# Loading the first chunk's weight words into two more buffers, an earlier residual load, and a chunk's closing steps one per unit, in an attention, DFT and feed-forward kernel

## The chip, the cores and the metric

The kernel runs on one core of one Trainium2 chip. The metric is the device time of one execution in microseconds (us). The core has a tensor engine (PE, with its own weight loads, PEld), a vector engine (DVE), a scalar engine (ACT), GpSimd (POOL), and SyncE (SP), on whose queue every transfer of this kernel is issued. Each engine works its own instructions in the order in which they stand, and waits at one whose inputs or buffers are not ready.

## The reference

q, k and v are (8, 12, 448, 64); the weights are 768 x 3072 and 3072 x 768.

```python
scores = scale * np.matmul(q, k.transpose(0, 1, 3, 2)) - np.log(S)
attn = 1.0 / (1.0 + np.exp(-scores))
x = attn @ v                      # heads side by side: (8, 448, 768)
X = np.fft.fft(np.fft.fft(x, axis=1), axis=2)
u = x + np.real(X).astype(np.float32)
un = (u - mean(u)) / np.sqrt(var(u) + 1e-06)      # over the last axis
out = (u + np.maximum(un @ w_ch1, 0.0) @ w_ch2).astype(np.float32)
```

The weights arrive as float64 words, that is, as pairs of 32-bit words, and are made into pairs of float16 tiles (a high part and a low part) on the chip.

## The kernel before

The 8 x 448 = 3584 tokens of the feed-forward part are seven chunks of 512. The work has four stages on the time line.

**Attention and DFT**, up to about 456 us, are not touched.

**The first chunk** (c = 0, 456 to 715 us): for each of the 24 blocks of 128 hidden units (f) there is `up_proj` (18 matmuls into `psh`), `evac` (ACT writes `hh`, L545; DVE writes `hl`, L546) and `down_proj` of the block before (24 matmuls into the six banks `po`). Beside it the weights are made. The list `order` names 48 weight blocks; `prep_step(k, n)` makes block k in four parts: SP loads the words of a later block into a buffer `wr` (L373), ACT takes an absolute value (`wt`, L382), DVE makes four passes (L384 to L392), ACT writes the high part (L400), SP stores `wt` to `t_dram` (L401), and DVE writes the low part one step later (L403). Two such steps stand in each block f. There are three `wr` buffers, and at step k the words of block k + 2 are loaded.

**The second chunk** (c = 1, 715 to 931 us) has the same three parts, and beside them two others. `combine(i, p, n)` makes 24 combined weight tiles for the fast chunks: n = 0 loads `cb` from `t_dram` (L619, in the `wr` buffers too), n = 1 is four adds on DVE (L627), n = 2 the high part `ch` on ACT (L631), n = 3 the low part `cl` on DVE (L636), n = 4 six stores. `made_at` says in which block each part of tile j stands: loads in f - 1, adds and `ch` in f, `cl` and stores in f + 1, with f = 1 + j - (j > 8) - (j > 16), so that blocks 9 and 16 have two tiles. `fast_norm` normalizes the rows of the third chunk, in two passes of 12 blocks each (f 0 to 11 and 11 to 22): statistics, 16 short DVE steps for the root, transposes on PE (`pst`, in blocks 6 to 8 and 17 to 19, each in one of the two buffers of `psh`), copies to `U` (L676) and to `ut` (L688, L692). `residual(c, g)` loads the rows `ur` that are added at the end (L570), again into the `wr` buffers; `finish` adds them to the banks `po` (L578) when the last `down_proj` has filled them, and stores the result (L582).

**The fast chunks** (c = 2 to 6, from 931 us) work in units: seven products up (`fast_up`, `psf`, L771), seven down (`fast_down`, `pso`, L822), in turn; `fast_unit` runs one product and then what `todo` holds for this unit. `later(d, fn)` puts a step d units ahead. Weights come by `load_w` into `ws` (L699), each in a unit of its own before it is used. A down product is added to `acc` on DVE (L831). In the last group of a chunk `fast_finish` follows each down product: eleven steps for each half of the tokens (seven adds, `add`, L846; four `put`, L850, of which two issue a store to `out`, L856). They stand in the unit of the product itself, so all eleven lie in six units in a row.

After each group `pin()` fixes the order on every engine as it is written.

Of the kernel before, what the change touches and what calls it, by code (L numbers as in the profile page):

```python
# [11 lines left out]
I32 = mybir.dt.int32  # L12
# [11 lines left out]
DM = 768  # L24
# [34 lines left out]
def spectral_attention_ffn(tc, q, k, v, w1, w2, cd, cs, ident_in, out):  # L59
# [8 lines left out]
    with ExitStack() as top:  # L68
# [19 lines left out]
        if True:  # L88
# [279 lines left out]

            def prep_w(i, f, n):

                if n == 0:
                    prep[i, f] = r = wpre.tile([128, DM, 2], I32, tag="wr", name="wr", bufs=3)
                    nc.sync.dma_start(  # L373
                        r.rearrange("p n w -> p (n w)"), (w1, w2)[i][:, f * 2 * DM:(f + 1) * 2 * DM])
                    return
# [30 lines left out]
            def prep_step(k, n):  # L406

                for d, m in (((2, 0), (-1, 4)), ((1, 1),), ((0, 2),), ((0, 3),))[n]:
                    if k + d < len(order) and (k + d, m) not in prepped:
                        prepped.add((k + d, m))  # L410
                        prep_w(*order[k + d], m)
# [108 lines left out]
        with ExitStack() as fast, ExitStack() as st, ExitStack() as early:  # L520
            un_pool = fast.enter_context(tc.tile_pool(name="un_pool", bufs=1))
            up = fast.enter_context(tc.tile_pool(name="up", bufs=2))
# [180 lines left out]
            for j in range(NFC):  # L703
                f = 1 + j - (j > 8) - (j > 16)
                made_at.setdefault(f - 1, []).append((j, 0))
                made_at.setdefault(f, []).extend((j, n) for n in (1, 2))
                made_at.setdefault(f + 1, []).extend((j, n) for n in (3, 4))
# [7 lines left out]
            for c in range(NPLAIN):  # L715
                for f in range(NFC):
                    if (c, f) not in hs:
                        up_proj(c, f)
                    for n in range(2):
# [4 lines left out]
                        if n == 0 and (c or f):  # L724
                            evac(c, f)
                    if c == NPLAIN - 1:
# [5 lines left out]
                    if f in (NFC - 3, NFC - 2) and c < NPLAIN - 1:  # L732
                        residual(c, f - NFC + 3)
                    if f == NFC - 1 and c == NPLAIN - 1:
                        residual(c, 0)
                        residual(c, 1)
# [104 lines left out]
            def fast_finish(c, tp, no):  # L841
# [16 lines left out]
                for x in {2: ((add, 2, 1), (put, 2, 0, 0)), 6: ((add, 6, 1),), 7: ((add, 7, 6),),  # L858
                          4: ((add, 4, 7), (put, 4, 1, 0)), 5: ((add, 7, 5), (add, 6, 5), (put, 7, 1, 1)),
                          3: ((add, 3, 6), (put, 3, 0, 1))}.get(no, ()):  # L860
                    later(0, lambda x=x: x[0](*x[1:]))
# [97 lines left out]
```

## Time and profile before

| what | value |
|---|---|
| time, median of 3 runs | 1811.45 us (1807.61 to 1819.85) |
| the profiled execution | 1808.63 us, its span 1806.8 us |
| PE busy | 1670.1 us (92%) |
| DVE busy | 1297.8 us (72%) |
| ACT busy | 603.1 us (33%) |
| DMA queue | 61.5% of 16 engines' span, 393.19 MB |
| mean granted PE clock | 0.977 |

The span is the time from the first to the last instruction of the profiled execution. A busy share is a mean over stages that differ, so the rows below go stage by stage. A wait in square brackets is idle time of that engine just before the row, with what ended it.

### The profile page before, as it was taken

The numbers are of one execution on the slowest core, as the hardware profiler recorded it, in microseconds if no ns is written. First come the engines' busy times: TensorE is split into PE (matmuls) and PEld (weight loads), VectorE is DVE, ScalarE is ACT, GpSimd is POOL, SyncE is SP. The second block draws the span as 40 slices with busy tenths as digits, with TensorE's granted clock in tenths as the row PEclk, the third lists the DMA queues.
The fourth block names the chain that finished last, engine by engine and source line by source line (L and its number), as shares of the span: only waits on it lengthen the run. The fifth ranks groups of instructions, "written<-read, shape, count | busy, mean of one in ns | idle before, by whom it ended". The sixth has DMA issues, their size and how long they took to land. (4 is left out here: it accounts for less than half of the span.)

```text
span 1806.8 us, 27683 instructions
## 1 busy us (share of the span) xinstructions
PE 1670.1 (92%) x10996; PEld 1069.6 (59%) x10996; DVE 1297.8 (72%) x2481; ACT 603.1 (33%) x767; POOL 193.6 (11%) x220
## 2 busy tenths in 40 slices
PE   8999999987777778999879999999999999999997
PEld 4555545543533334555447777677777767776774
DVE  4445576656777776567656888788868887887667
ACT  5444444434333332133224332333133323232221
POOL 4534344334000000000000000000000000000000
PEclk9999999998999999999989999999999999999999
DMA  7666676654666665588887563756476546556551
GB/s 243 214 207 220 222 229 219 207 167 117 217 211 211 211 212 195 182 280 309 294 303 266 227 245 145 280 202 231 152 284 224 217 178 254 216 205 249 215 223 62
DMA packets 109139, 394.95 MB, mean 219 GB/s; under 512 B 23521, under 2 KB 49362, under 8 KB 93522
## 3 DMA queue, kind: packets, MB, share of 16 engines
q1 hardware_dynamic: 109010, 393.19, 61.5%
q8 instruction: 86, 1.41, 0.3%
q14 instruction: 43, 0.35, 0.1%
HBM read 316.08 MB, written 73.92 MB: 216 GB/s over the span
## 5 line engine op out<-in xcount | busy, mean ns | idle before, releaser
L771 PE MATMUL psf<-ut,ws 128*128 128x256 f16 x3780 | 425.4, 274 | 21.4 <-DMA ws<-w_dram 11.7
L822 PE MATMUL pso<-ws,H 128*128 128x384 f16 x2520 | 423.9, 326 | 4.5 <-DVE X L777 1.8
L771 PEld LDWEIGHTS <-ws 128*128 128x128 f16 x3780 | 370.8, 98 | 74.2 <-DMA ws<-w_dram 14.8
L822 PEld LDWEIGHTS <-H 128*128 128x128 f16 x2520 | 246.3, 98 | 160.8 <-issue 5.4
L136 ACT ACTIVATE a<-sc 112x900 f32<-112x900 f32 x192 | 166.8, 918 | 157.0 <-PE sc L132 156.9
L831 DVE TENSOR_TENSOR acc<-pso,acc 128x384 f32<-128x384 f32 x350 | 183.6, 550 | 18.8 <-PE pso L822 18.8
L796 ACT ACTIVATE F<-F 128x1024 f32<-128x1024 f32 x60 | 63.5, 1058 | 357.1 <-DVE F L777 357.1
L557 PE MATMUL po<-w2h,hh 128*128 128x512 f16 (+1 forms) x384 | 131.8, 343 | 52.0 <-ACT hh L545 51.3
L152 PE MATMUL av<-a,vr 112*64 112x450 f32 x768 | 171.1, 568 | 3.8 <-DVE xT L161 3.8
L777 DVE TENSOR_TENSOR H<-F,H 128x1024 f16<-128x1024 f32 x120 | 129.5, 1087 | 48.1 <-ACT H L806 48.1
L538 PE MATMUL psh<-ut,w1h 128*128 128x512 f16 x504 | 151.2, 382 | 3.0 <-DVE hl L546 3.0
L557 PEld LDWEIGHTS <-hh 128*128 128x128 f16 x768 | 76.6, 102 | 108.6 <-ACT hh L545 61.1
L777 DVE TENSOR_TENSOR F<-X,psf 128x256 f32<-128x256 f32 x240 | 96.8, 419 | 51.8 <-PE psf L771 48.0
L557 PE MATMUL po<-w2h,hl 128*128 128x512 f16 (+1 forms) x384 | 130.8, 341 | 1.9
L806 ACT ACTIVATE H<-F 128x1792 f16<-128x1792 f32 x60 | 101.8, 1697 | 88.7 <-DVE F L777 88.7
L557 PE MATMUL po<-w2l,hh 128*128 128x512 f16 (+1 forms) x384 | 131.2, 342 | 0.0
L161 DVE TENSOR_SCALAR xT<-av 128x450 f32<-128x450 f32 x48 | 30.1, 626 | 136.2 <-PE av L152 136.2
L777 DVE TENSOR_TENSOR F<-F 128x256 f32<-128x256 f32 x240 | 91.2, 422 | 24.5 <-ACT F L796 20.5
L132 PE MATMUL sc<-qh,kh 64*112 64x450 f32 x384 | 82.2, 424 | 18.0 <-ACT a L136 13.4
L546 DVE SCALAR_TENSOR_TENSOR hl<-psh,hh 128x512 f16<-128x512 f32 x48 | 33.1, 690 | 90.5 <-ACT hh L545 90.5
L152 PEld LDWEIGHTS av<-a,vr 112*64 112x64 f32 x768 | 47.7, 139 | 82.7 <-issue 67.8
L538 PE MATMUL psh<-ut,w1l 128*128 128x512 f16 x252 | 96.1, 382 | 0.0
(89 smaller groups left out, 1954.9 us busy)
## 6 DMA issues: line engine op xcount, KB each, us to landing
ws<-w_dram SPq DMA_DIRECT2D x120, 1344.0 KB, 8.8
wr<-w_in SPq DMA_DIRECT2D x96, 768.0 KB, 4.9
t_dram<-wt SPq DMA_DIRECT2D x48, 384.0 KB, 2.3
cb<-t_dram SPq DMA_DIRECT2D x24, 768.0 KB, 5.3
qr<-q_in SPq DMA_DIRECT2D x48, 225.0 KB, 3.7
kr<-k_in SPq DMA_DIRECT2D x48, 224.0 KB, 3.4
vr<-v_in SPq DMA_DIRECT2D x24, 448.0 KB
w_dram<-ch SPq DMA_DIRECT2D x24, 384.0 KB, 5.8
```

Source lines behind the costliest of these rows:

```text
L132: nc.tensor.matmul(ps[:CP, j, :SQ], split[g, 1, kn][h, c * CP:(c + 1) * CP], split[g, 0, qn][h], start=(n == 0), stop=(n == 2))
L136: nc.scalar.activation(a, ps[:CP, :, :SQ], AF.Sigmoid, bias=-math.log(S), scale=1.0 / math.sqrt(D))
L152: nc.tensor.matmul(ps[j * D:(j + 1) * D, :SQ], vr[:, c, h * D:(h + 1) * D], a[:, j], start=(c == 0), stop=(c == 3))
L538: nc.tensor.matmul(hs[c, f], l[f][:, m], r[:, m], start=(m == n == 0), stop=(m == NCC - 1 and n == 2))
L546: nc.vector.scalar_tensor_tensor(out=hl, in0=ps, scalar=0.0, in1=hh, op0=ALU.max, op1=ALU.subtract)
L557: nc.tensor.matmul(po[n][:, at:at + hi - lo], l[:, cols], r[f][:, lo:hi], start=(f == 0 and m == 0 and at == 0), stop=(f == NFC - 1 and m ...
L771: nc.tensor.matmul(ps[:, :TH], w[:, x, a, m * 128:(m + 1) * 128], ut[y][:, b, m], start=(m == n == 0), stop=(m == n == 2))
L777: nc.vector.tensor_tensor(out=o, in0=x, in1=y, op=op)
L796: nc.scalar.activation(F[:, 0:4], F[:, 0:4], AF.Relu)
L806: nc.scalar.activation(hts[P][:, 0], F[:, 1:8], AF.Copy)
L822: nc.tensor.matmul(ps[:, :384], H[:, x, a, tp * 128:(tp + 1) * 128], w[:, y, b], start=(j == n == 0), stop=(j == 1 and n == 2))
L831: later(0, lambda: nc.vector.tensor_tensor(out=to, in0=ps[:, :384], in1=to, op=ALU.add))
```

## The change

It has four edits. Two more buffers, one tile called `spare`, are made in `un_pool`, which stands empty until the second chunk; blocks k >= 8 of the weight list with k % 5 > 2 load into them, and `prep_step` issues a load as soon as the block that held its buffer is done, up to four blocks ahead. In the second chunk `made_at` has four blocks with two tiles (5, 8, 11 and 14) in place of two (9 and 16), so the last tile is done two blocks sooner. The residual of the second chunk is loaded in blocks 21 and 22, ahead of the other steps of the block, and no longer in block 23. The closing steps of fast chunks 2 to 5 stand one to a unit in the eleven units after the last down product; those of the last chunk stay.

```diff
--- before.py
+++ after.py
@@ -366,10 +366,26 @@
             for f in range(NFC):
                 order += [(1, f)] + [(0, f + NPRE)] * (f + NPRE < NFC)
 
+            spare = []
+
+            def in_spare(k):
+                return k >= 8 and k % 5 > 2
+
+            def loadable(k, done):
+
+                here = [j for j in range(k) if in_spare(j) == in_spare(k)]
+                n = 2 if in_spare(k) else 3
+                return len(here) < n or here[-n] < done
+
             def prep_w(i, f, n):
 
                 if n == 0:
-                    prep[i, f] = r = wpre.tile([128, DM, 2], I32, tag="wr", name="wr", bufs=3)
+                    k = order.index((i, f))
+                    if in_spare(k):
+                        r = spare[0][:, k % 5 - 3]
+                    else:
+                        r = wpre.tile([128, DM, 2], I32, tag="wr", name="wr", bufs=3)
+                    prep[i, f] = r
                     nc.sync.dma_start(
                         r.rearrange("p n w -> p (n w)"), (w1, w2)[i][:, f * 2 * DM:(f + 1) * 2 * DM])
                     return
@@ -405,7 +421,12 @@
 
             def prep_step(k, n):
 
-                for d, m in (((2, 0), (-1, 4)), ((1, 1),), ((0, 2),), ((0, 3),))[n]:
+                loads = []
+                for d in range(2, 5):
+                    if not loadable(k + d, k):
+                        break
+                    loads.append((d, 0))
+                for d, m in ((*loads, (-1, 4)), ((1, 1),), ((0, 2),), ((0, 3),))[n]:
                     if k + d < len(order) and (k + d, m) not in prepped:
                         prepped.add((k + d, m))
                         prep_w(*order[k + d], m)
@@ -519,6 +540,7 @@
 
         with ExitStack() as fast, ExitStack() as st, ExitStack() as early:
             un_pool = fast.enter_context(tc.tile_pool(name="un_pool", bufs=1))
+            spare.append(un_pool.tile([128, 2, DM, 2], I32, tag="U", name="spare"))
             up = fast.enter_context(tc.tile_pool(name="up", bufs=2))
             wp = early.enter_context(tc.tile_pool(name="wp", bufs=1))
             ps_h = st.enter_context(tc.tile_pool(name="ps_h", bufs=2, space=PSUM))
@@ -701,7 +723,7 @@
 
             norm_at, made_at = {}, {}
             for j in range(NFC):
-                f = 1 + j - (j > 8) - (j > 16)
+                f = 1 + j - (j > 4) - (j > 8) - (j > 12) - (j > 16)
                 made_at.setdefault(f - 1, []).append((j, 0))
                 made_at.setdefault(f, []).extend((j, n) for n in (1, 2))
                 made_at.setdefault(f + 1, []).extend((j, n) for n in (3, 4))
@@ -723,17 +745,14 @@
                             slot += 1
                         if n == 0 and (c or f):
                             evac(c, f)
+                    if f in (NFC - 3, NFC - 2):
+                        residual(c, f - NFC + 3)
                     if c == NPLAIN - 1:
                         for j, n in made_at.get(f, ()):
                             combine(j % 2, j // 2, n)
                     if c == NPLAIN - 1:
                         for tp, n in norm_at.get(f, ()):
                             fast_norm(NPLAIN, tp, n, ps_h)
-                    if f in (NFC - 3, NFC - 2) and c < NPLAIN - 1:
-                        residual(c, f - NFC + 3)
-                    if f == NFC - 1 and c == NPLAIN - 1:
-                        residual(c, 0)
-                        residual(c, 1)
                     if prev is not None:
                         down_proj(*prev)
                     prev = (c, f)
@@ -855,10 +874,15 @@
                     elif n == 1:
                         nc.sync.dma_start(out[r0:r0 + 128, :], u[:, k])
 
-                for x in {2: ((add, 2, 1), (put, 2, 0, 0)), 6: ((add, 6, 1),), 7: ((add, 7, 6),),
-                          4: ((add, 4, 7), (put, 4, 1, 0)), 5: ((add, 7, 5), (add, 6, 5), (put, 7, 1, 1)),
-                          3: ((add, 3, 6), (put, 3, 0, 1))}.get(no, ()):
-                    later(0, lambda x=x: x[0](*x[1:]))
+                steps = {2: ((add, 2, 1), (put, 2, 0, 0)), 6: ((add, 6, 1),), 7: ((add, 7, 6),),
+                         4: ((add, 4, 7), (put, 4, 1, 0)), 5: ((add, 7, 5), (add, 6, 5), (put, 7, 1, 1)),
+                         3: ((add, 3, 6), (put, 3, 0, 1))}
+                if c == NCK - 1:
+                    for x in steps.get(no, ()):
+                        later(0, lambda x=x: x[0](*x[1:]))
+                elif no == 3:
+                    for n, x in enumerate(x for k in (2, 6, 7, 4, 5, 3) for x in steps[k]):
+                        later(1 + n, lambda x=x: x[0](*x[1:]))
 
             def fast_unit(fn, *args):
                 fn(*args)
```

**SP's queue, the end of the second chunk.** `ur` is the residual, `ch`, `cl`, `w2h`, `w2l`, `w1h` and `w1l` are sources of stores of combined weights, `ws` the fast chunks' weights. Before:

```order
L699 DMA ws<-w_dram 128x5376
L649 DMA w_dram<-ch 128x1536
L650 DMA w_dram<-w2h_4500 128x768
L651 DMA w_dram<-w2h_4499 128x384
L649 DMA w_dram<-cl 128x1536
L650 DMA w_dram<-w2l_4521 128x768
L651 DMA w_dram<-w2l_4520 128x384
L570 DMA ur<-u_dram 128x2x768 x2
L582 DMA y_out<-ur 128x2x768 x2
L699 DMA ws<-w_dram 128x5376 x5
```

Now:

```order
L721 DMA ws<-w_dram 128x5376
L592 DMA ur<-u_dram 128x2x768
L671 DMA w_dram<-ch 128x1536
L672 DMA w_dram<-w2h_4503 128x768
L673 DMA w_dram<-w2h_4502 128x384
L671 DMA w_dram<-cl 128x1536
L672 DMA w_dram<-w2l_4524 128x768
L673 DMA w_dram<-w2l_4523 128x384
L592 DMA ur<-u_dram 128x2x768
L721 DMA ws<-w_dram 128x5376
L604 DMA y_out<-ur 128x2x768 x2
L721 DMA ws<-w_dram 128x5376 x5
```

The two residual loads stood one after the other behind the last stores; now the first stands ahead of the last tile's six stores, and the second behind them.

**SP's queue, the end of the first fast chunk.** `y_out` is the output. Before:

```order
L839 DMA ur<-u_dram 128x768 x2
L699 DMA ws<-w_dram 128x5376 x4
L856 DMA y_out<-ur 128x768 x2
L699 DMA ws<-w_dram 128x5376 x2
L856 DMA y_out<-ur 128x768 x2
L699 DMA ws<-w_dram 128x5376 x2
L659 DMA U<-u_dram 128x768 x2
```

Now:

```order
L858 DMA ur<-u_dram 128x768 x2
L721 DMA ws<-w_dram 128x5376 x6
L875 DMA y_out<-ur 128x768 x2
L721 DMA ws<-w_dram 128x5376 x2
L875 DMA y_out<-ur 128x768 x2
L681 DMA U<-u_dram 128x768 x2
```

Each pair of output stores has moved behind two more weight loads.

**DVE, blocks 4 to 6 of the second chunk** (`U` is the rows' scaling in block 4, `hl` begins a block). Before:

```order
L323 TENSOR_SCALAR U<-U,mv 128x768 x2
L546 SCALAR_TENSOR_TENSOR hl<-psh,hh 128x512
L636 SCALAR_TENSOR_TENSOR cl<-cb,wsc,ch 128x1536
L627 TENSOR_TENSOR cb<-cb 128x384 x4
L546 SCALAR_TENSOR_TENSOR hl<-psh,hh 128x512
L636 SCALAR_TENSOR_TENSOR cl<-cb,wsc,ch 128x1536
L627 TENSOR_TENSOR cb<-cb 128x384 x4
```

Now:

```order
L323 TENSOR_SCALAR U<-U,mv 128x768 x2
L568 SCALAR_TENSOR_TENSOR hl<-psh,hh 128x512
L658 SCALAR_TENSOR_TENSOR cl<-cb,wsc,ch 128x1536
L649 TENSOR_TENSOR cb<-cb 128x384 x8
L568 SCALAR_TENSOR_TENSOR hl<-psh,hh 128x512
L658 SCALAR_TENSOR_TENSOR cl<-cb,wsc,ch 128x1536 x2
L649 TENSOR_TENSOR cb<-cb 128x384 x4
```

Block 5 has two sets of four adds, and block 6 two low parts.

## Rows read from the trace of the kernel before

**Rows 1.** Windows: length; busy PE, PEld, DVE, ACT, POOL; PE clock; DMA share; GB/s.

```profile
456.00:715.00 259.00, 203.00 (x987) 102.40 (x987) 198.50 (x263) 89.92 (x116) 2.93 (x2) 0.93 0.61 207
715.00:931.00 216.00, 210.46 (x1137) 111.89 (x1136) 140.51 (x232) 61.77 (x72) 0.00 (x0) 0.99 0.79 277
```

**Rows 2.** Waits, 480 to 715 us: total us, times, longest.

```profile
PE po L557 <- ACT hh L545: 51.3, 20, 7.8
...
ACT wt L382 <- DMA wr<-w_in: 4.5, 3, 2.9
```

**Rows 3.** Waits of PE, 735 to 931 us.

```profile
PE psh L538 <- DVE hl L546: 3.0, 1, 3.0
PE pst L675 <- ACT U L676: 2.5, 2, 2.3
```

**Rows 4.** Timelines, 925 to 949 us: start, us, engine, instruction, [idle before].

```profile
929.41 1.34 SPq L570 DMA_DIRECT2D ur<-u_dram  x2
...
936.42 4.29 DVE L578 SCALAR_TENSOR_TENSOR ur<-po,wsc,ur 128x512 f32<-128x512 f32 x8 [8.92 <-DMA ur<-u_dram]
...
940.77 8.62 PE L771 MATMUL psf<-ut,ws 128*128 128x256 f16 x64 [9.70 <-DVE ur L578]
```

**Rows 5.** Windows of 10 us, the one behind this wait.

```profile
940.00:950.00 10.00, 9.23 (x72) 7.71 (x72) 3.58 (x9) 0.61 (x2) 0.00 (x0) 0.81 0.76 278
```

**Rows 6.** The chain that ended last: one set of seven products up.

```profile
1097.06 6.89 PE psf L771 x63
```

**Rows 7.** Waits of PE, 1090 to 1665 us.

```profile
PE psf L771 <- DMA ws<-w_dram: 11.7, 8, 2.3
PE pso L822 <- DVE X L777: 1.8, 4, 0.4
PE pso L822 <- DVE acc L831: 1.6, 2, 0.9
```

**Rows 8.** Timeline of SP at the first chunk end.

```profile
1116.77 2.05 SPq L856 DMA_DIRECT2D y_out<-ur  x2
```

**Rows 9.** Timeline of ACT, 486 to 492 us.

```profile
488.81 0.94 ACT L382 ACTIVATE wt<-wr 128x768 f32<-128x768 f32 x1 [2.88 <-DMA wr<-w_in]
490.06 0.93 ACT L400 ACTIVATE w2h<-wt,wsc 128x768 f16<-128x768 f32 x1 [0.32 <-DVE wt L392]
```

**Rows 10.** Timeline of ACT, second chunk, blocks 3, 4, 10 and 11.

```profile
757.23 0.60 ACT L545 ACTIVATE hh<-psh 128x512 f16<-128x512 f32 x1 [0.88 <-PE psh L538]
...
765.01 0.60 ACT L545 ACTIVATE hh<-psh 128x512 f16<-128x512 f32 x1 [0.89 <-PE psh L538]
...
823.00 2.98 ACT L688 ACTIVATE ut<-U 128x384 f16<-128x384 f32 x7
825.89 0.57 ACT L545 ACTIVATE hh<-psh 128x512 f16<-128x512 f32 x1
```

**Rows 11.** Groups, 735 to 931 us: instruction, count; busy us, mean ns; idle before.

```profile
L627 DVE TENSOR_TENSOR cb<-cb 128x384 f32<-128x384 f32 x96 | 53.4, 557 | 6.5 <-DMA cb<-t_dram 3.9
L636 DVE SCALAR_TENSOR_TENSOR cl<-cb,wsc,ch 128x1536 f16<-128x1536 f32 x24 | 43.4, 1810 | 0.2 <-DMA w_dram<-ch 0.2
...
L317 DVE TENSOR_SCALAR mv<-mv 128x2 f32<-128x2 f32 x8 | 1.4, 169 | 0.3
```

**Rows 12.** Timelines of ACT and PE, second chunk, blocks 17 and 18.

```profile
873.44 0.58 ACT L545 ACTIVATE hh<-psh 128x512 f16<-128x512 f32 x1
...
874.80 0.59 PE L538 MATMUL psh<-ut,w1h 128*128 128x512 f16 x2 [3.03 <-DVE hl L546]
```

**Rows 13.** Tile `cb`, 735 to 931 us: its loads, from issue to landing.

```profile
DMA to landing us min/median/max: 4.5/5.3/6.1
```

**Rows 14.** Groups of instructions, 960 to 1807 us.

```profile
L846 DVE TENSOR_TENSOR acc<-acc 128x384 f32<-128x384 f32 x70 | 38.2, 557 | 2.1
```

**Rows 15.** Windows, 28 units inside a fast chunk.

```profile
1069.66:1097.06 27.40, 27.40 (x212) 20.53 (x211) 23.22 (x51) 9.17 (x13) 0.00 (x0) 1.00 0.62 231
```

**Rows 16.** Timeline of PE at the second chunk end.

```profile
1314.55 8.61 PE L771 MATMUL psf<-ut,ws 128*128 128x256 f16 x62 [2.28 <-DMA ws<-w_dram]
```

## The prediction, made before the change was timed

> **What bounds the kernel now.** I read the windows first, stage by stage, then who waited for whom in each, then the timelines around the longest waits. Three stages matter.
>
> In the first chunk neither PE nor DVE is full: PE is busy 203 of 259 us, DVE 198.5 [rows 1]. PE's waits there are 51.3 us in 20 pieces, all for ACT's `hh` [rows 2], which stands in ACT's queue behind a weight step's high part, and that behind DVE's four passes. ACT and DVE hand work to each other, and that chain sets the pace.
>
> In the second chunk PE is the bound: 210.46 of 216 us [rows 1]. It loses 3.0 us once and 2.5 us in two waits [rows 3]. At its end stands the longest wait of PE that the change concerns: the residual is issued at 929.41, DVE sits idle 8.92 us until it lands and then adds eight pieces in 4.29 us, and the first product of the third chunk begins 9.70 us late [rows 4]. In the window behind this wait the granted clock is 0.81 [rows 5], a mixture of 1.2 and 2.4 GHz after an idle engine: 64 products take 8.62 us [rows 4] where 63 take 6.89 inside a chunk [rows 6].
>
> In the fast chunks PE waits only at the four chunk ends: 11.7 us in eight waits for `ws`, 1.8 us in four for DVE's X and 1.6 us in two for `acc`, 15.1 us in all [rows 7]. SP shows why: two output stores are issued at 1116.77 and after [rows 8], once DVE has made what they carry, and the weight loads stand behind them in the queue.
>
> **The change part by part.** *Loads up to four blocks ahead.* There are as many loads as before, on the same queue, waiting for the same event: with five buffers that of block k + 4 is freed by block k - 1, as that of k + 2 was with three. So SP is held no longer, and a load lands two steps sooner. What that can give is ACT's wait for the words, 4.5 us in three waits [rows 2]. The longest, 2.88 us, ends at 488.81; its instruction takes 0.94 us, to 489.75, and the next one starts at 490.06 because DVE's last pass ended then [rows 9]. The load was late, and nobody behind it was. Bounds: 4.5 us saved, 0, or a loss if the two loads that now go ahead of the last stores of u held those up, which nobody reads for 200 us. I take 0, the value of the longest wait.
>
> The Trainium skill ("Perfetto Trace Analysis", Optimization Strategy) says that the same gap, repeated on an engine that should be saturated, can mean too little SBUF for the next tile. By it PE's 20 repeated gaps would shrink with two more buffers, which is rival 4; the trace disagrees, since the rows name ACT's `hh` as what ended them.
>
> *The residual in blocks 21 and 22.* It lands at least a block before it is needed. DVE can then begin when the first of six banks is full: a block lasts 7.78 us (two starts of `hh` that wait for PE, 757.23 and 765.01 [rows 10]), its down half 3.89, a bank 0.65. DVE's 4.29 us begin 3.24 us ahead of PE's end and end 1.05 behind it; with the hand-over some 1.3 of the 9.70 us stay. That saves 8.4 us, and the products behind it 1.6 (8.62 less 7.00, 64 at the rate of [rows 6]): 10.0 us. The `wr` buffers that it takes are those of tiles 21 and 22, which the new places finish by block 20, so SP is not held there.
>
> *Tiles packed closer.* That room is bought by four double blocks in place of two. In a block with one tile `hh` waits 0.89 us for PE [rows 10]: the chain `hh`, `hl`, `cl`, four adds, `ch`, next `hh` takes 6.89 us, and 0.89 is all its slack. A second tile adds four adds of 0.557 us, 2.23 [rows 11], so `hh` falls back 1.34; the next block has a second `cl` of 1.81 [rows 11] and loses 0.92 more. A single block gives 0.89 back. Of `fast_norm`, seven copies on ACT cost 2.98 [rows 10]; 16 short steps of 0.17 us [rows 11], 0.2 apart, cost 3.3 less the two that ACT's `ch` and `hh` take anyway, 1.3. A transposing block lasts 0.44 longer on PE, and its copy on ACT as long.
>
> This account can be tried on the trace. In block 11 `hh` starts at 825.89; on time it would be at 757.23 + 8 x 7.78 + 3 x 0.44 = 820.8, so it is 5.1 late [rows 10]. The account gives 1.34 (double block 9) + 0.92 + 2.98 = 5.2. In block 17 it starts at 873.44 against 867.5, 5.9 late, and PE then waits 3.03 us [rows 12], because a transpose has taken the other buffer. So in a transposing block 2.9 are free; in others about 6.7, since the down half that needs `hl` comes a whole block after the up half.
>
> Now the new order. After block 5 `hh` is 1.3 late, after block 6 2.3, and the transpose of block 7 needs the copy that stands behind the late `ch`: PE waits about 2.5, and the lateness is gone. After block 8: 1.3. After 9: 2.3. After 10, with the seven copies: 4.4. After 11: 5.7. After 12: 6.6. After 13: 5.7. After 14: 7.1. After 15, with its second `cl` and the short steps of block 14: 9.3. PE pays what is over 6.7, 2.6 in blocks 15 and 16. Block 16 gives 0.89 back, and in transposing block 17 a lateness of 5.8 costs PE 2.9, and the copy behind it 2.1, as it cost 2.3 before [rows 3]. Sum 10.1 us, against 5.5 now [rows 3]: 4.6 lost. DVE's waits for `cb`, 3.9 us now [rows 11], should grow, since two loads in a row land one after the other: up to 4 more. Bounds 0 (all of it where PE has slack) and 9; I take 7, nearer the upper end, because a landing takes 4.5 to 6.1 us [rows 13] of a chain of 6.89.
>
> *Closing steps one to a unit.* No instruction is added. Eleven steps of some 0.557 us [rows 14], 6.1 us, come on top of DVE's 23.22 us in 28 units, 11.6 in 14 that last 13.7 [rows 15]. So a half's closing puts DVE 4.0 us behind. Before, two halves follow each other: 8 us, and the eight PSUM buffers, seven units or 6.9 us, run out. Now the second half's steps lie in 14 units where ACT writes `acc` in DVE's place and takes 7 x 0.55 off it: 11.6 - 3.9 + 6.1 = 13.8, and the debt stays at 4. On SP the stores wait for DVE's units 22 and 24, then 36 and 38; the weight load behind the first pair is used from unit 42, some 14 us on, where PE's longest wait for one is now 2.3 us [rows 7]. All of the 15.1 us can go, and with them the stretch at a lower clock behind one wait, 62 products in 8.61 us [rows 16] for 6.8: 1.8. I take 17; bounds 8 (half, if a load is late still) and 17.
>
> **Sum.** 0 + 10 - 7 + 17 = 20 us. The profiled execution took 1808.6 us, so 1788.6. It lies 2.8 us below the median of the runs shown, 1811.45, by which it is 1791.5. I say 1790.
>
> **The rivals.**
> 1. *The packing is hidden.* For it: block 9 is double now and PE loses nothing there. Against it: double block 16 precedes all of PE's 5.5 us, and block 5 has the same neighbours. Then 27 us are saved: 1783.
> 2. *The chunk ends keep half,* because loads held behind the stores arrive late in another unit. For it: SP is still held twice per chunk end. Against it: the 14 us of lead. 0 + 10 - 7 + 8 = 11 saved: 1799.
> 3. *The packing costs double,* 14 us, by waits for `cb` and by stretches at 1.2 GHz: 1797.
> 4. *The gaps of the first chunk are a matter of buffers.* Then up to 51.3 us more go [rows 2]: about 1739. Against it [rows 9].
> 5. *Slower.* The loads of `cb` become the pace of the second chunk. At a landing of up to 6.1 us [rows 13] they already hold DVE at times [rows 11], so by an estimate from these rows a block lasts its load's landing plus 1.7 us (7.78 at 6.1). At 8 us each it is 9.7, and 20 blocks lose 38 us: 27 less 38, 1822. It decides from 7.5 on, where the loss passes the 27 us of the rest. For it: the DMA share there is 0.79 [rows 1], and packing raises it. Against it: no landing above 6.1.
>
> **How the numbers follow.** About 1% (18 us) is what a measurement of this kernel can tell from no change. Forecast 0.56, its own range 1784 to 1797 by the bounds of the packing and of the ends; rival 1 0.15; rival 2 0.15; rival 3 0.06; rival 4 0.04; rival 5 0.04. The line of 1% lies at 1793.3. Below it are two thirds of the forecast (0.38), rivals 1 and 4 and a fifth of 2 (0.22), together 0.60; within 1% 0.36; slower 0.04. The range takes in rivals 1 to 3: 1779 to 1801.
>
> **What would show it.** Before the third chunk's first product PE's wait for `ur` should be 1.3 us or so. At the chunk ends no wait for `ws`, X or `acc` should be left. In the second chunk PE should wait for `hl`, `hh` and `U` in blocks 7 and 15 to 18, some 10 to 14 us in all. In the first, ACT's waits for words should be gone and its 259 us unchanged. I would be wrong by most if the second chunk's lateness is smaller than the account, or if a late weight load appears inside a fast chunk.

## The result, and the profile after

The changed kernel takes 1796.67 us (median of five runs, 1793.55 to 1797.58); the kernel before took 1812.26 in the same comparison (1807.61 to 1819.85). The ratio of the runs is 0.9896, with a 95% interval of 0.9877 to 0.9916: 18.8 us of 1812 (15.2 to 22.3), where 20 were forecast. The two medians differ by 15.6 us.

The profiled execution of the changed kernel has a span of 1795.1 us, 11.7 less than before. One reason why that is less than 18.8 is that the stage ahead of the first chunk lasts a different time in each execution: the second block's `hh` starts at 495.98 in the profile of before and at 498.12 in that of after, and over the thirteen profiles of this study in which the chunk's weight steps stand in their old order it starts between 495.0 and 506.0 (497.2 to 501.9 in the five with the loads ahead). So stages are compared here, not spans. From the second block's `hh` on, the three stages together are 13.8 us shorter in this pair of profiles. Some 3.5 us of what is missing to 18.8 may lie in the second chunk of the changed kernel's profile, as the windows beside no_loads below suggest; no profile shows a place for the rest.

The windows of the first chunk, of the second chunk from its first `hh` to the first product of the fast chunks, and of the fast chunks. Columns as in [rows 1]. After:

```profile
456.00:715.00 259.00, 203.59 (x989) 102.99 (x988) 198.73 (x265) 89.19 (x115) 3.91 (x3) 0.93 0.61 208
735.91:950.21 214.30, 197.57 (x1039) 103.42 (x1038) 142.06 (x236) 59.45 (x68) 0.00 (x0) 0.97 0.77 273
950.21:1795.10 844.89, 833.18 (x6396) 627.32 (x6395) 685.39 (x1544) 251.31 (x330) 0.00 (x0) 1.00 0.59 221
```

The last two stages of before, cut at the same marks:

```profile
733.81:940.77 206.96, 191.72 (x1039) 102.19 (x1037) 141.81 (x236) 59.53 (x68) 0.00 (x0) 0.97 0.81 283
940.77:1806.80 866.03, 839.02 (x6396) 628.14 (x6395) 692.10 (x1544) 251.38 (x330) 0.00 (x0) 0.99 0.57 215
```

The first chunk is what it was [rows 1]: PE 203.59 of 259 us. The second chunk is 7.34 us longer, although the wait for the residual at its end has gone. The fast chunks are 21.14 shorter. In both, PE's busy time moved as well as its idle time, for the same count of products: 5.85 us more in the second chunk, 5.84 less in the fast ones. A product that runs behind a pause at a lower granted clock is busy longer, as 64 behind the wait for the residual were [rows 4] beside 63 inside a chunk [rows 6]. So a wait can cost more than its length, but not each one does: of the eight waits for `ws` before, only the longest, 2.28 us, has products at the lower clock behind it [rows 16].

Waits of PE after, in the first chunk (480 to 715 us, beside [rows 2]), the second (735 to 960, beside [rows 3]) and the fast chunks (955 to 1795, beside [rows 7]):

```profile
PE po L579 <- ACT hh L567: 50.5, 20, 7.8
...
PE psh L560 <- DVE hl L568: 5.0, 1, 5.0
PE po L579 <- ACT hh L567: 4.2, 2, 3.6
PE pst L697 <- ACT U L698: 3.2, 2, 2.9
PE po L579 <- DVE hl L568: 1.5, 1, 1.5
PE pst L697 <- DVE hl L568: 1.4, 1, 1.4
PE psf L790 <- DVE ur L600: 1.1, 1, 1.1
...
PE pso L841 <- DVE H L796: 0.8, 1, 0.8
```

Fifty us of waits in the first chunk stay where they were; ACT's waits for the words [rows 2] are gone from the list of that stretch, and nothing came of it. In the second chunk the waits for `hh`, `hl` and `U` grew from 5.5 to 15.3 us. At the chunk ends the waits for `ws`, X and `acc`, 15.1 us, are gone. The 0.8 us for H stand at the head of the first fast chunk; the kernel before waits 0.76 us there too, at 964.89, ahead of the stretch of [rows 7].

The hand-over to the fast chunks, in the timelines of SP, DVE and PE, beside [rows 4]:

```profile
930.80 0.56 SPq L592 DMA_DIRECT2D ur<-u_dram  x1
...
945.86 4.29 DVE L600 SCALAR_TENSOR_TENSOR ur<-po,wsc,ur 128x512 f32<-128x512 f32 x8 [3.23 <-PE po L579]
...
950.21 4.96 PE L790 MATMUL psf<-ut,ws 128*128 128x256 f16 x44 [1.13 <-DVE ur L600]
```

The second residual load is issued 15 us before DVE needs it. DVE waits for PE now and no longer for a load, and PE's wait is 1.13 us where it was 9.70.

### The profile page after: what moved, and what is told of

Read it like the earlier page. It is cut to its first block, busy times and chain, and to the rows that moved or that the text cites. A ratio compares the mean times of both kernels' runs of the same rounds, so it can differ in the third digit from the quotient of the medians.

```text
span 1795.1 us, 27673 instructions
## 1 busy us (share of the span) xinstructions
PE 1671.5 (93%) x10996; PEld 1070.2 (60%) x10996; DVE 1290.0 (72%) x2481; ACT 602.4 (34%) x767; POOL 194.3 (11%) x220
## 5 line engine op out<-in xcount | busy, mean ns | idle before, releaser
L796 DVE TENSOR_TENSOR F<-F 128x256 f32<-128x256 f32 x240 | 91.2, 421 | 17.7 <-ACT F L815 13.7
```

Of the source, the lines that this page charges most:

```text
L796: nc.vector.tensor_tensor(out=o, in0=x, in1=y, op=op)
```

## The experiments

Each kernel was timed against the kernel before on the same chip. This table holds the stages of the profiled executions: the first chunk from the second block's `hh` to the second chunk's first `hh`, the second chunk from there to the first product `psf`, the fast chunks from there to the end of the span. Each stage comes from one execution. Where the order of a stage is the same, it differs by some us: the second chunk takes 206.36 to 208.30 in before, ends_only, stores_later and loads_only, and the fast chunks 861.04 and 864.00 in pack_resid and resid_only.

| kernel | ratio to before (95%) | first chunk | second | fast |
|---|---|---|---|---|
| before | 1 | 237.83 | 206.96 | 866.03 |
| after | 0.9896 (0.9877 to 0.9916) | 237.79 | 214.30 | 844.89 |
| ends_only | 0.9911 (0.9893 to 0.9930) | 238.79 | 206.36 | 846.59 |
| resid_only | 0.9942 (0.9922 to 0.9961) | 237.75 | 199.83 | 864.00 |
| pack_resid | 1.0015 (0.9997 to 1.0033) | 237.75 | 210.52 | 861.04 |
| loads_only | 1.0023 (1.0009 to 1.0038) | 239.44 | 208.30 | 865.28 |
| no_pack | 0.9837 (0.9820 to 0.9853) | 237.81 | 201.64 | 844.88 |
| late_double | 0.9838 (0.9816 to 0.9860) | 237.81 | 203.09 | 846.59 |
| no_loads | 0.9881 (0.9857 to 0.9904) | 237.83 | 210.76 | 844.91 |
| two_parts | 0.9830 (0.9802 to 0.9858) | 237.81 | 201.71 | 845.88 |
| stores_later | 0.9941 (0.9928 to 0.9955) | 237.80 | 206.89 | 856.65 |
| ch_later_packed | 0.9832 (0.9816 to 0.9848) | 237.79 | 202.09 | 844.95 |
| ch_later | 0.9791 (0.9771 to 0.9811) | 237.80 | 192.15 | 845.29 |
| both_chains | 0.9482 (0.9452 to 0.9512) | 184.70 | 191.65 | 845.20 |

**Each part alone.** *ends_only*: of the change's diff, the piece with `steps` and `later(1 + n, ...)`.

> The kernel before with the closing steps one to a unit, nothing else. My theory: the third chunk's first product to the end took 866.0 us before and 844.9 in the changed kernel, 1.6 of it products behind the wait for the residual at the lower clock; so this part alone gives 19.5 us, a ratio near 0.989, and no wait for ws, X or acc at any chunk end. Rival (the parts help each other: the weight loads at the chunk ends come early only because the loads ahead or the earlier residual freed the queue): 8 to 10 us, a ratio near 0.995, and half of the 11.7 us for ws stays.

Measured 0.9911, 16 us; in the trace the fast chunks are 19.4 us shorter and the one wait of PE in them is the 0.8 us for H that the kernel before has too. The rival falls: no wait for `ws` is left without the other parts.

*resid_only*: the residual earlier, the tiles where they were.

```diff
-                    if f in (NFC - 3, NFC - 2) and c < NPLAIN - 1:
+                    if f in (NFC - 3, NFC - 2):
                         residual(c, f - NFC + 3)
-                    if f == NFC - 1 and c == NPLAIN - 1:
-                        residual(c, 0)
-                        residual(c, 1)
```

> The kernel before with the second chunk's residual in blocks 21 and 22 behind the tiles' steps there, and the tiles where they were. My theory: the earlier load needs no packing; PE's wait for ur falls from 9.70 to about 1.1 us and the products behind it run at full clock, 10 us saved, ratio 0.9945, and PE's 5.5 us of waits for hl and U in the second chunk stay as they were. Rival (the room bought by the packing is needed, since the buffers of tiles 21 and 22 come free late): the second residual load lands after PE's last product, 3 to 6 us of the wait stay, and the ratio is 0.997 or nearer to 1.

Measured 0.9942, 10.5 us (9.2 by the second chunk and the fast chunks of its trace). PE's waits up to the fast chunks:

```profile
PE psh L538 <- DVE hl L546: 3.0, 1, 3.0
PE pst L675 <- ACT U L676: 2.8, 1, 2.8
PE psf L768 <- DVE ur L578: 1.1, 1, 1.1
```

The wait for `ur` is that of the changed kernel, without a tile moved. So the room that the packing buys is not needed.

*pack_resid*: the pieces of the diff for `made_at` and the residual.

> The kernel before with the four double blocks and the earlier residual as in the change, nothing else. My theory: the packing costs 15.9 us (9.8 of waits, the rest stretches behind them at a granted clock under 1) and the residual gives 10.2 back, so this part alone is 5.7 us slower, ratio 1.003, with PE's waits in the second chunk near 15 us. Rival (what the second chunk lost in the changed kernel comes from the loads ahead, which leave the DMA queues later): no loss, PE's waits there near 5.5 us, and 10 us faster, ratio 0.9945.

Measured 1.0015, no gain and no clear loss, where the residual alone gave 10.5 us: the packing costs 13 us by the ratios (0.0073 of 1811) and 10.7 by the second chunk (210.52 against 199.83). PE's waits there are those of the changed kernel, 15 us. The rival, that the loads ahead had lengthened the second chunk, falls.

*loads_only*: the pieces of the diff with `spare`, `in_spare` and `loadable`.

> The kernel before with the loads up to four blocks ahead, nothing else. My theory: ACT's 4.5 us of waits for the words go and nothing else moves; the blocks of the first chunk stay 11.22 us apart, ratio 1.000 within 0.002. Rival (the medians of both kernels differ by 15.6 us and the spans of their profiled executions by only 11.7, and the runs of the changed kernel lie closer together, so the loads take a delay away that comes in some executions): 4 us faster, ratio 0.998, and a smaller spread than the 12 us of the kernel before.

Measured 1.0023, 4.2 us slower (1.6 to 6.9), with no smaller spread (1810 to 1818). The first chunk's blocks stay 11.22 us apart. The rival falls. In the trace the first chunk is 1.6 us longer, at its end, and the second 1.3; but ends_only, without these loads, has a first chunk 1.0 longer too, and four of the five kernels with them have not. So where the small loss arises is not shown.

**Parts taken out of the change.** *no_loads*: the changed kernel without those pieces.

> The changed kernel without the loads up to four blocks ahead. My theory: those loads are worth nothing or cost the 4.2 us (interval 1.6 to 6.9) that they cost alone, so this is equal to the changed kernel or faster, ratio 0.987 to 0.9896. Rival (parts one by one add up to only 9 us of the 19 that the change gave, so the loads help where the other parts stand beside them): slower than the changed kernel by 4 us or more, ratio 0.992 or above.

Measured 0.9881, not told apart from the changed kernel's 0.9896. With it the sum question is answered by stages: 210.76 and 844.91 us are what pack_resid and ends_only show, the latter less the slow products behind `ur`. Parts add up in the trace to some us; the ratios of single kernels add up only within their intervals. The second chunk of the changed kernel's profile is the exception, with 214.30 us. Here are the windows of pack_resid and of no_loads:

```profile
737.04:947.56 210.52, 194.17 (x1039) 102.09 (x1037) 141.93 (x236) 59.33 (x68) 0.00 (x0) 0.98 0.78 278
732.83:943.59 210.76, 194.02 (x1038) 102.14 (x1037) 141.87 (x236) 59.35 (x68) 0.00 (x0) 0.98 0.79 277
```

PE is idle as long as in the changed kernel (16.35 and 16.74 us, there 16.73), but its products are busy 3.4 and 3.55 us less, at a clock of 0.98 where it was 0.97. Whether the loads ahead did this or the one execution is not shown.

*no_pack*: the changed kernel with two double blocks.

```diff
-                f = 1 + j - (j > 4) - (j > 8) - (j > 12) - (j > 16)
+                f = 1 + j - (j > 8) - (j > 16)
```

(and the residual loads behind the tiles' steps, as in resid_only)

> The changed kernel with the tiles of the kernel before (double blocks 9 and 16 alone) and the residual loads behind the tiles' steps of blocks 21 and 22. My theory: packing is pure loss, 13.2 us by the two kernels that had the residual with and without it (ratios 1.0015 and 0.9942); so this beats the changed kernel by as much, ratio near 0.982 to the kernel before, PE's waits in the second chunk near 7 us with the one for ur at 1.1. Rival (the loss was a matter of those executions, or a late residual load eats it): within 0.003 of the changed kernel's 0.9896.

Measured 0.9837, 10.7 us below the changed kernel; the second chunk is 12.66 shorter. The two intervals do not meet, so the packing, with the place of the residual loads, is a loss in this kernel as well.

*two_parts*: resid_only and ends_only together.

> The kernel before with the closing steps one to a unit and the residual in blocks 21 and 22 behind the tiles' steps; no packing, no loads ahead. My theory: 16.1 and 10.5 us add up, ratio 0.9853, or up to 0.982 if the changed kernel's own 19 us for fast chunks and the products behind ur counts; the same as with the loads ahead, or up to 4 us faster. Rival (the loads ahead help beside the others): 4 us or more slower than the kernel without packing.

Measured 0.9830, the same as no_pack. For the loads ahead there are now three comparisons (alone, beside the packing, without it), and none shows a gain. With no_loads it compares the packing once more: 9.1 us by the second chunk (210.76 against 201.71), 9.3 by the ratios.

**Where the packing's cost arises.** *late_double*: in no_pack the second double block is 20 in place of 16, `(j > 20)`.

> As the one without packing, but the second double block is 20 and not 16. My theory, the lateness account: block 16's second tile and the short steps ahead of it make hh late in the transposing blocks 17 and 18, where only 2.9 us are free; from block 20 on nothing transposes and 6.7 are free, so PE's waits for hl and U, 5.5 us, and the slow stretch behind them go: 4 to 7 us less than without packing, ratio 0.978 to 0.980. Rival (the lateness collects over the chunk whatever the place, and the last blocks push DVE into the end): the wait moves to blocks 20 to 23 or to ur, and the ratio is that of the kernel without packing, 0.982, or above.

Measured 0.9838: nothing gained. PE's and DVE's waits show the rival's picture; the two for `hh` end at 929.02 and 935.86 us, in the last two blocks:

```profile
PE po L579 <- ACT hh L567: 3.5, 2, 2.6
PE psf L790 <- DVE ur L600: 2.3, 1, 2.3
PE pst L697 <- ACT U L698: 2.0, 1, 2.0
PE psh L560 <- DVE hl L568: 1.3, 1, 1.3
...
DVE cl L658 <- DMA w_dram<-ch: 4.9, 2, 4.6
```

The wait for `hl` shrank, but a wait for `ur` grew and `cl` waited 4.6 us for a store. I had no term for that last wait. `ch` and `cl` share three buffers of the tag `wt`; two tiles in one block need four, so the second `cl` has to wait until the first `ch` has been stored.

*ch_later_packed*: the changed kernel, with ACT's `ch` a block later and right behind `hh`. DVE's and SP's orders do not change.

```diff
-                made_at.setdefault(f, []).extend((j, n) for n in (1, 2))
-                made_at.setdefault(f + 1, []).extend((j, n) for n in (3, 4))
+                made_at.setdefault(f, []).append((j, 1))
+                made_at.setdefault(f + 1, []).extend((j, n) for n in (2, 3, 4))
...
-                x.sort(key=lambda x: (x[1] < 3, x[1] > 0, x))
+                x.sort(key=lambda x: (x[1] < 2, x[1] > 0, x))
```

> The changed kernel with each tile's high part on ACT moved from the block of its four adds to the block behind, right after hh; the orders of DVE and SP are untouched. My theory: packing costs because the next hh stands on ACT behind ch, and ch behind DVE's adds, so a second set of adds puts hh late; with ch behind hh instead nothing on ACT waits for the adds of its own block, PE's waits in the second chunk fall from 15 us to under 3 and the slow stretches with them, and the change's ratio of 0.9896 goes to about 0.982. Rival (the packing costs by the loads of cb, whose wait on DVE doubled, and by the stores that hold cl's buffer): DVE is as late as before, PE's waits stay over 8 us, the ratio at 0.987 or above.

Measured 0.9832; the second chunk fell from 214.30 to 202.09 us. PE's waits in it, and DVE's for loads and stores:

```profile
PE po L579 <- DVE hl L568: 5.2, 3, 3.6
PE psh L560 <- DVE hl L568: 2.5, 1, 2.5
PE psf L790 <- DVE ur L600: 1.1, 1, 1.1
...
DVE cb L649 <- DMA cb<-t_dram: 10.0, 10, 3.1
DVE cl L658 <- DMA w_dram<-ch: 6.8, 3, 3.6
```

The ratio is what I expected, the waits are not: 7.7 us stay, not under 3. No wait of PE ends with ACT any more, and all that are left but the one for `ur` end with DVE's `hl`. Some of these stand behind DVE's waits for `cb` and for `wt`'s buffers; in others ACT is late again, because a `ch` ahead of `hh` waits for a store (here `hh` follows at 853.93, and PE waits 1.15 us for its `hl` at 855.28):

```profile
852.45 1.58 ACT L653 ACTIVATE ch<-cb,wsc 128x1536 f16<-128x1536 f32 x1 [4.52 <-DMA w_dram<-w1l]
```

So the order on ACT was worth 12 us beside the changed kernel's profile, and 8 to 9 beside pack_resid and no_loads, which have the changed kernel's order in this chunk. What packing still costs with the new order, 10 us by the second chunk (202.09 against the 192.15 of the next kernel) and 7 by the ratios, is not shown to come from DVE's waits by themselves: in the next kernel DVE waits 10.7 us for `cb` and 5.1 for stores, nearly as long.

*ch_later*: the same move in two_parts.

> The same move in the kernel with two double blocks, the residual in blocks 21 and 22 and the closing steps one to a unit (its ratio without the move was 0.983). My theory: the 5.5 us that PE waited in the second chunk before the change, and some 2 us of slow products behind them, were the same chain; they go, ratio 0.979, the second chunk 194 to 196 us from its first hh to the third chunk's first product where it was 201.7. Rival (those waits come from the transposes' two buffers): they stay, ratio 0.983.

Measured 0.9791, the second chunk 192.15 us, below the 194 to 196 expected. PE is busy 189.76 of them, at a granted clock of 1.00:

```profile
740.96:933.11 192.15, 189.76 (x1039) 101.91 (x1038) 142.06 (x236) 59.36 (x68) 0.00 (x0) 1.00 0.84 297
```

With the same two PSUM buffers the waits for `U` are gone; the rival falls. The second chunk is 9.6 us shorter than in two_parts; by the ratios it is 7, and the two intervals just overlap. DVE still waits for the loads of `cb`, as long as in the packed kernel, but PE waits for `hl` only 1.3 us:

```profile
DVE cb L627 <- DMA cb<-t_dram: 10.7, 7, 3.3
```

**What the spread closing steps did.** *stores_later*: the kernel before, where DVE's closing steps stay packed and only the stores on SP go ten units later.

```diff
-                        nc.sync.dma_start(out[r0:r0 + 128, :], u[:, k])
+                        later(10, lambda: nc.sync.dma_start(out[r0:r0 + 128, :], u[:, k]))
```

> The kernel before, with the output stores of the chunk ends issued ten units later than the step that ends their rows, and DVE's closing steps packed as they were. My theory, as the prediction has it in two parts: the 11.7 us of waits for ws come from weight loads that stand behind stores on SP, so they go, and with them most of the stretch at lower clock; the 3.4 us for X and acc come from DVE's debt and stay: 11 to 13 us faster, ratio 0.993 to 0.9945. Rival (DVE's debt is the whole cause: the weights' buffers come free late too because PE is held): the waits move from ws to X and acc, 5 us or less are gained, ratio 0.997 or above.

Measured 0.9941, 10.7 us; the fast chunks are 9.4 us shorter. PE's waits in them:

```profile
PE pso L822 <- DVE acc L831: 6.0, 8, 0.9
PE pso L822 <- DVE X L777: 1.8, 4, 0.4
PE pso L822 <- DVE H L777: 0.8, 1, 0.8
```

No wait for `ws` is left: those were the stores ahead of them in SP's queue. But the waits for `acc` grew from 1.6 to 6.0 us, so part of DVE's debt had been hidden behind the waits for `ws`. Of the part's 19 us about half comes with the queue of SP, the rest only when DVE's steps are spread too.

**The same idea in the first chunk.** *both_chains*: ch_later, and in the first chunk a new order inside each weight step `k`. Before: load `k + 2`, low part of `k - 1`, absolute values of `k + 1`, two passes of `k`, two passes and high part of `k`; `hh` and `hl` behind the first step of a block. Now:

```diff
+                        steps = ((2, 0), (0, 2), (-1, 4), (1, 1), (0, 3)) if c == 0 and slot <= len(order) else ()
+                        for i, (d, m) in enumerate(steps):
+                            if i == 3 and n == 0 and f:
+                                evac(c, f)
...
-                        if n == 0 and (c or f):
+                        if n == 0 and (c or f) and not steps:
                             evac(c, f)
```

> The kernel with the high parts of the second chunk a block later, two double blocks, the earlier residual and the closing steps one to a unit (ratio 0.9791), and in the first chunk the same idea: in each weight step the previous step's low part goes behind this step's first two passes, and hh and hl stand ahead of the step's absolute values, last two passes and high part; no buffer is added. My theory: the first chunk's 11.22 us per block are the hand-overs of ACT and DVE to each other, 2.5 us per block in which DVE is idle (1.00 behind the high part, 1.49 behind hh); with other work in between, DVE's 8.72 busy us per block are what is left, blocks lie 8.8 to 9.3 us apart, some 20 of them, and 38 to 48 us go: ratio 0.953 to 0.958. Rival (the gaps of the first chunk are a matter of buffers or of the words' loads, as rival 4 of the prediction has it): blocks stay 11.2 us apart, ratio 0.979. Between them (the hand-overs move to another place in the same ring): about 10 us per block, 0.967.

Measured 0.9482: 1717.73 us (1712.0 to 1724.88) beside 1812.19 for the kernel before. The first chunk went from 237.8 to 184.70 us, and the block ahead of it, from the first `hh` to the second, from 35.6 in the kernel before to 30.8. In the timelines two `hh` of ACT and what DVE does around the first of them, without a gap:

```profile
564.20 0.58 ACT L545 ACTIVATE hh<-psh 128x512 f16<-128x512 f32 x1
572.56 0.58 ACT L545 ACTIVATE hh<-psh 128x512 f16<-128x512 f32 x1
...
564.33 1.02 DVE L403 SCALAR_TENSOR_TENSOR w2l<-wt,wsc,w2h 128x768 f16<-128x768 f32 x1
565.26 0.68 DVE L546 SCALAR_TENSOR_TENSOR hl<-psh,hh 128x512 f16<-128x512 f32 x1
565.87 0.95 DVE L390 SCALAR_TENSOR_TENSOR wt<-wr,wt 128x768 int32<-128x768 int32 x1
```

The same two DVE instructions in the kernel before, each behind a hand-over from ACT:

```profile
603.34 1.02 DVE L403 SCALAR_TENSOR_TENSOR w2l<-wt,wsc,w2h 128x768 f16<-128x768 f32 x1 [1.00 <-ACT w2h L400]
...
608.89 0.69 DVE L546 SCALAR_TENSOR_TENSOR hl<-psh,hh 128x512 f16<-128x512 f32 x1 [1.49 <-ACT hh L545]
```

And the windows of 150 us in the middle of the chunk, now and before:

```profile
505.00:655.00 150.00, 143.53 (x760) 72.78 (x759) 147.52 (x198) 73.04 (x89) 0.00 (x0) 1.00 0.80 274
```

```profile
540.00:690.00 150.00, 117.25 (x560) 55.67 (x561) 113.40 (x148) 53.48 (x68) 0.00 (x0) 0.93 0.63 212
```

A block takes 8.36 us where it took 11.22, DVE is busy 147.52 of 150 us, and the granted clock is 1.00 where it was 0.93. That is more than the 38 to 48 us expected: I had taken 8.8 to 9.3 us per block, and left out the block ahead of the chunk. It is the fastest kernel here, faster than the kernel before and the changed one. ACT now waits 26.4 us in 22 pieces for the words, so the loads ahead might be worth something in this order; that was not tried.

## Why the prediction was right, and where its terms were off

The forecast of 1790 us was 6.7 below the measured median, inside its range, and the sign and the size of the gain came out: 20 us forecast, 18.8 by the ratio. Of the four terms two were right and two were too small: the packing cost more than forecast, and the chunk ends gave more in this trace. That these two errors work against each other, and the total came out nearer than the packing's term, is luck.

- *Loads up to four blocks ahead*, 0. Right: ACT's waits for the words are gone and the first chunk is the same to 0.1 us. By the ratio alone they cost 4.2 us, beside the other parts nothing that can be told.
- *The residual in blocks 21 and 22*, 10.0. Right: 10.5 by the ratio of resid_only, 9.2 by its trace; PE's wait is 1.13 us where 1.3 was forecast.
- *Tiles packed closer*, 7 with bounds of 0 and 9. This term was mis-sized: 12.66 us by the second chunk (after against no_pack), 10.7 by the ratios. The other comparisons give 10.7 by the second chunk and 13 by the ratios (pack_resid and resid_only), and 9.1 and 9.3 (no_loads and two_parts). So it cost 9 to 13 us, from the upper bound on. PE's waits for `hh`, `hl` and `U` are 15.3 us where 10 to 14 were forecast. Of the 12.66, 3.17 are products busy longer (197.57 against the 194.40 that the window of no_pack shows), and 9.49 is idle time. The account was near at first. From the rows below, on time being 7.78 us after the block before, `hh` of block 6 is 1.64 late (1.3 forecast) and that of block 7 3.07 (2.3), and the transpose waits 2.87 (2.5):

```profile
774.89 0.60 ACT L567 ACTIVATE hh<-psh 128x512 f16<-128x512 f32 x1 [0.44 <-PE psh L560]
784.31 0.58 ACT L567 ACTIVATE hh<-psh 128x512 f16<-128x512 f32 x1
793.52 0.59 ACT L567 ACTIVATE hh<-psh 128x512 f16<-128x512 f32 x1
...
793.67 1.11 PE L697 MATMUL pst<-ident,U 128*128 128x128 f32 x4 [2.87 <-ACT U L698]
```

Then it missed two things. The first is the wait for `wt`'s buffer. It holds the second `cl` behind double block 11, and block 13's `hh` with it, where the account had PE pay nothing between blocks 7 and 15:

```profile
850.70 1.82 DVE L658 SCALAR_TENSOR_TENSOR cl<-cb,wsc,ch 128x1536 f16<-128x1536 f32 x1 [3.23 <-DMA w_dram<-ch]
...
856.91 0.39 PE L579 MATMUL po<-w2h,hh 128*128 128x512 f16 x1 [3.59 <-ACT hh L567]
```

The second is the lowered clock, priced for the residual and for one wait of the chunk ends but not here. Windows of 10 us around the waits of 2.87, 3.59 and 5.0 us:

```profile
790.00:800.00 10.00, 7.13 (x26) 3.58 (x25) 5.77 (x9) 2.54 (x3) 0.00 (x0) 0.66 1.01 336
850.00:860.00 10.00, 6.29 (x27) 2.74 (x26) 6.38 (x7) 2.06 (x2) 0.00 (x0) 0.89 1.01 359
...
890.00:900.00 10.00, 4.98 (x16) 1.90 (x15) 6.73 (x10) 2.91 (x3) 0.00 (x0) 0.83 0.91 329
```

How much of this comes with the packing is open, since pack_resid and no_loads have the same idle time and lose 3.4 and 3.55 us less. The waits for `cb` grew as said: 7.8 us from 3.9, 3.9 more where up to 4 were forecast. But they did not set the size: in ch_later_packed they are 10.0 us, and the second chunk is 12 us shorter.

- *Closing steps one to a unit*, 17 with bounds of 8 and 17. Mis-sized by a little: 21.14 us less the 1.6 behind `ur` are 19.5 in the trace, 16.1 by the ratio of ends_only. Two other pairs give 16.1 and 18.1 in the trace (pack_resid and no_loads, resid_only and two_parts). The waits were counted rightly, but for the 0.76 us for H that stay, where the text says that PE waits only at the chunk ends. The lowered clock was counted rightly too, 1.8 us behind one wait. PE's busy time is 5.84 us less, and 1.6 of this are the products behind `ur`; what the sum left out is the rest, some 2.5 us. pack_resid shows it. Its chunk ends are packed as before and PE waits 13.7 us at them, but up to 1790 us no window of 1 us of its fast chunks has a granted clock below 0.97, and PE is busy 2.55 us longer than the 833.18 of the changed kernel:

```profile
947.56:1808.60 861.04, 835.73 (x6396) 626.47 (x6395) 691.78 (x1544) 251.29 (x330) 0.00 (x0) 1.00 0.57 217
```

Products overlap in the trace. 63 in a row take 6.89 us [rows 6], 0.109 each, but from the start of the first to the end of the last it is 7.05, here in the kernel before:

```profile
1142.56 7.05 PE L771 MATMUL psf<-ut,ws 128*128 128x256 f16 x63 [1.92 <-DMA ws<-w_dram]
```

So the last product ends 0.16 us after the next one could have started, and only from there on the profile counts a wait. For the 14 waits of [rows 7] that makes 2.2 us. The row also shows products at the full rate behind a wait of 1.92 us. That DVE's debt and SP's queue both matter is shown by stores_later; the text had them side by side as 3.4 and 11.7, but with the queue cleared the debt alone makes PE wait 7.8 for `acc` and X.

*The range.* The forecast's own range of 1784 to 1797 does not follow from its bounds: 10 - 9 + 8 = 9 us saved give 1801 as its upper end. The measured 1796.67 lies inside by either.

*The rivals.* Rival 1, packing hidden, is wrong. Rival 2, chunk ends that keep half, is wrong: no wait is left at them. Rival 3, packing at 14 us by waits for `cb` and stretches at 1.2 GHz, is nearer in size than the forecast by the changed kernel's profile (12.66) and right on the stretches; its waits for `cb` are not the cause, as ch_later_packed shows. That its 1797 is the measured median is luck, since the chunk ends gave more than it had. Rival 5 is wrong: the landings of `cb` take 4.7 to 6.4 us, far from 7.5. Rival 4, buffers in the first chunk, is wrong too: with two more buffers PE's 20 gaps are 50.5 us, as they were. both_chains shows what the gaps were: the same buffers in another order leave 10.7 us of them. The Trainium skill ("Perfetto Trace Analysis", Optimization Strategy), which says that gaps of this kind can mean too little room for the next tile, is not borne out here; these runs speak for the page's paragraph before it, to look at what ends the gap.

What stays open: why the loads ahead cost 4.2 us by themselves; what packing still costs PE when `ch` stands a block later; why the same waits lose 3.4 us more to the clock in one profile than in two others; and what makes the stage ahead of the first chunk end up to 11 us apart from one execution to the next.

## What to carry to other kernels

When two engines hand tiles to each other in a ring, read for each gap what ended it and what stood ahead of that on its queue; moving independent work in between gave 56 us here (0.9791 to 0.9482) without a buffer, and two more buffers gave nothing. A change that buys room for one stall by packing work elsewhere should first be tried without the packing: the earlier load alone gave its 9 to 10 us, and the packing cost 9 to 13. When a stall of PE is priced, add to its length the overlap with the next product that is lost, 0.16 us here for each wait; and add a stretch at the lower clock, from rows, as a range from nothing up, since only some of the waits had one behind them.

## What the runs showed of the hardware

- A short wait of PE can cost more than its length. In the second chunk the same 1,038 or so products and transposes are busy 189.76 us when PE is idle 2.39 us in all (ch_later), with a granted clock of 1.00; when it is idle 16.35 to 16.74 us, they are busy 194.02 and 194.17 (no_loads, pack_resid, 0.98) or 197.57 (after, 0.97).
- The lower clock does not follow each wait. At the chunk ends of the kernel before it follows one wait for `ws` of eight, the longest (62 products in 8.61 us behind 2.28); the 63 products behind 1.92 take 7.05 us. In pack_resid, which waits 13.7 us there, the longest time 1.7, it follows none.
- The time to the first chunk's second `hh` differs by up to 11 us (495.0 to 506.0) between the executions of these kernels, while the first chunk behind it repeats to 0.1 us in eleven of these thirteen profiles (237.75 to 237.83).
